# Other groups of the first weight loads, an order table solved anew, and two casts moved to GpSimd in an attention and MoE kernel

## The chip, the cores and the metric

The kernel runs on one core of one Trainium2 chip. The metric is the device time of one execution in microseconds (us). The time given for a kernel is the median of its runs. Before the change it was 302.77 us (three runs, 302.61 to 303.33). A difference below 2% (6 us) counts as "same".

## The reference, cut to what matters

```python
# q, k, v: 8 batches x 8 heads x 576 tokens x 64
q_s = softmax(q, axis=-1)              # over the 64 features
k_s = softmax(k, axis=2)               # over the 576 tokens
kv  = einsum('bhsd,bhse->bhde', k_s, v)
x   = einsum('bhsd,bhde->bhse', q_s, kv)      # then reordered to 4608 tokens x 512
h   = x @ w_in                         # 512 -> 2048   ("W1" in the kernel)
g   = where(h > 0, h, exp(min(h, 0)) - 1)
out = g @ w_out                        # 2048 -> 512   ("W2")
```

(The reference subtracts the maxima ahead of the exponentials; the kernel, with its small inputs, does not.)

## The kernel before: what the change and the argument touch

The attention is worked in 16 *units* (a batch, and half of its heads), the MoE in 9 *blocks* of 512 tokens. For a unit ScalarE takes the exponentials of q and k and casts v to bf16 (tile VB); VectorE sums and scales q (tile QS); q is transposed (tile qsT, by TensorE for the first units, by a DMA afterwards); TensorE makes kv (VB and k), VectorE normalizes it into MBLK, TensorE multiplies qsT with it, and the result is copied to XT, the input of the MoE. For a block TensorE multiplies XT with W1, ScalarE (ESB) and VectorE (ESB, GT) work out the ELU, TensorE multiplies GT with W2, and ScalarE or VectorE copies the result to an output buffer (OSB) from which it is stored.

All operations are created in program order and numbered. In what order an engine executes them is not decided when the program runs: it is a fixed table of those numbers, one row for each engine.

```python
BYDMA = 4
CASTS = 4
ORDER = {
    "pe":  ("30 28 32 45 43 47 50 68 54 67 70 71 69 72 82 86 93 103 115 128 90 129 ..."),
    "act": ("3 22 33 23 31 24 34 29 44 35 48 55 73 76 77 79 83 84 87 94 95 104 97 ..."),
    # ... rows for VectorE, GpSimd and the queue of SyncE ("sp")
}
```

A small model of the machine walks through the table. It decides one thing only: where TensorE is thought to idle after 9.4 us, and how many *warm-up* matmuls (128x128, on the identity, result unused) are put there.

```python
SPIN_FROM = 9400.0
def fill(self, seq):
    out, free, done = [], self.SPIN_FROM, False
    for o in seq:
        if o.eng == "pe" and not done:
            idle = o.start - free - 150
            count = int(idle / 80)
            if count > 1 and all(d.end < free for d in self.spare_after):
                # ... an op of `count` warm-up matmuls, which waits for the identity alone
            free = o.end
            done = o is self.spare_until
        out.append(o)
```

The loads of W1 (groups of 256 columns; the first groups cut into two halves of the contraction), the casts, and the output buffers:

```python
for g0, g1, half in ((0, 3, 0), (0, 3, 1), (3, 5, None), (5, 8, None)):
    self.load_w1(g0, g1, half, -30, [gate, self.ident] if half == 0 else ())

def first(n, what="qk"):                    # the first work of unit n
    def go():
        self.stage1(n, due(n), what=what, vconv="gp" if n < CASTS else "act")
        # ...

def widen(self, n, key):                    # qsT of unit n from its transposed bf16 form
    # ...
    if n < CASTS:   # on GpSimd
        # ...
    else:           # on ScalarE

def out_store(self, jb, ts, bk, key, eng="act"):
    if jb == 0:
        i, osb = f"x{ts}", self.OSB0[ts]    # block 0: four buffers of its own (OSBX)
    else:
        i = self.oslot % len(self.OSB)      # afterwards a ring of three (OSB)
        # ... copy the bank to the buffer, then two stores of 64 rows (128 KB) each
```

`widen` is only called for units from `BYDMA` = 4 on, so its GpSimd branch was never taken. The q, k and v loads of the later units and the stores are issued by one engine, SyncE, in the order of the table's row "sp".

The softmax here doesn't subtract the row's maximum and nothing guards it: scores larger than these inputs give would overflow.

## Time and profile before

| | before |
|---|---|
| median of 3 runs | 302.77 us |
| profiled run, span in the trace | 302.01 us, 300.2 us |
| first transpose on TensorE | 8.91 us |
| full clock rate, by the trace's clock record | 11.94 us |
| first W1 matmul | 15.42 us |
| last matmul starts | 296.27 us |

In the profile PE is TensorE, DVE VectorE, ACT ScalarE, POOL GpSimd, SPq the queue of DMAs that SyncE issues. "L545" is a line of the program. As the matmuls are issued by helper functions, it pays to learn five of them: L406 transposes, L458 kv, L489 attention output, L545 W1, L590 W2; L655 are the warm-ups. After the change the same lines are L403, L456, L487, L543, L588 and L653. A *hole* below is the time by which the starts of two neighbouring matmuls lie further apart than is usual for that shape (0.227 us for 128x512); it is about 0.16 us larger than the idle time that the profile reports, since the record of one such matmul lasts 0.39 us (those of before just ahead of 53 us), longer than the usual step to the next start.

Two lines of the page of the kernel before: the busy time of each engine, and the chain of waits that ended last.

```profile
PE 286.4 (95%) x1855; PEld 234.2 (78%) x1855; DVE 189.0 (63%) x244; ACT 182.7 (61%) x213; POOL 20.2 (7%) x31
...
PE 88%; ACT 6%; DMA 3%; DVE 2%; issue 0%; SPq 0%
```

TensorE is the bound: it is busy for 95% of the span, and 88% of the last chain is its own work. Then its waits between 15 and 280 us (who waits for whom: us in all, how often, longest).

```profile
PE PS L545 <- ACT OSBX L607: 0.6, 1, 0.6
PE PS L458 <- ACT XT L511: 0.4, 1, 0.4
```

After the start-up there is 0.6 us to be had, at one place. That place and the start-up in TensorE's timeline (start, duration, what; in brackets the idle time ahead of it and what ended it), first at 8 to 16 us:

```profile
8.91 1.14 PE L406 MATMUL PS<-ID,QS 128*128 128x128 f16 x9 [8.91 <-DVE QS L383]
9.84 2.13 PE L655 MATMUL PS<-ID 128*128 128x128 f16 x18
...
12.32 0.68 PE L406 MATMUL PS<-ID,QS 128*128 128x128 f16 x9
...
15.42 0.74 PE L545 MATMUL PS<-XT,W 128*128 128x512 f32 x2
```

Nine transposes took 1.14 us at 8.91 and 0.68 us at 12.32, their starts 107 and 56 ns apart: in between, at 11.94, the full rate of the clock record begins. And at 52 to 61 us:

```profile
52.28 1.07 PE L545 MATMUL PS<-XT,W 128*128 128x512 f32 x4
53.90 3.94 PE L545 MATMUL PS<-XT,W 128*128 128x512 f32 x16 [0.55 <-ACT OSBX L607]
...
59.13 0.78 PE L458 MATMUL PS<-VB,KR 64*64 64x65 bf16 x72
```

The 0.55 us wait for ScalarE's copy of block 0's output (a hole of 0.71 us) is the largest after the start-up. The kv product of units 4 and 5 follows at 59.13.

### The profile page before, as it was taken

To read this page: it belongs to the slowest core of one execution; us is meant where nothing else is said; L and a number is where in the kernel's file an instruction comes from. 1 tells how busy PE (TensorE), PEld (TensorE's weight loads), DVE (VectorE), ACT (ScalarE), POOL (GpSimd) and SP (SyncE) were. 2 spreads that over 40 slices of the span, in tenths; PEclk is the share of its full clock that TensorE was granted. 3 is DMA by queue.
4 is the path that set the end of the run, shared out by engine and by line. 5 is a ranking of instruction groups with operands and counts; after the bars stand their busy time and mean duration, and the time that the engine had idled before them with its cause. 6 is when DMAs were issued, how large, how long until landed. Compare 5 with 4: busy or idle time off the path is not lost.

```text
span 300.2 us, 4428 instructions
## 1 busy us (share of the span) xinstructions
PE 286.4 (95%) x1855; PEld 234.2 (78%) x1855; DVE 189.0 (63%) x244; ACT 182.7 (61%) x213; POOL 20.2 (7%) x31
## 2 busy tenths in 40 slices
PE   0799999999999999999999999999999999999995
PEld 0678887777888888888888878888888888888883
DVE  3858934987896596787687567675344546356500
ACT  5858759988976889668937664555441543233311
POOL 0950343000000000000000000000000000000000
PEclk9999999999999999999999999999999999999998
DMA  7999999795769697368477730324030032111133
GB/s 265 385 400 388 391 340 328 232 215 211 214 154 330 177 244 218 81 213 291 131 174 180 212 114 2 75 57 107 0 86 2 0 72 60 27 36 36 35 88 87
DMA packets 35283, 49.96 MB, mean 166 GB/s; under 512 B 16320, under 2 KB 16320, under 8 KB 35264
## 3 DMA queue, kind: packets, MB, share of 16 engines
q1 hardware_dynamic: 29680, 34.09, 41.1%
q0 software_dynamic: 5504, 15.47, 15.9%
q8 instruction: 14, 0.23, 0.3%
q10 hardware_dynamic: 80, 0.13, 0.1%
q14 instruction: 5, 0.04, 0.0%
HBM read 36.70 MB, written 9.44 MB: 154 GB/s over the span
## 4 chain that ended last, share of the span: by engine, by line
PE 88%; ACT 6%; DMA 3%; DVE 2%; issue 0%; SPq 0%
PE PS L590 41%; PE PS L545 41%; PE PS L489 3%; PE PS L458 2%; DMA out_dram<-OSB 2%; ACT QR L355 1%; DMA QR<-in_q_dram 1%; ACT ESB L561 1%; PE PS L406 1%; ACT VB L368 1%; ACT KR L359 1%; PE PS L655 1%; ACT OSB L607 1%; DVE QS L383 0%; DVE ZQ L375 0%; ACT XT L511 0%
## 5 line engine op out<-in xcount | busy, mean ns | idle before, releaser
L590 PE MATMUL PS<-W,GT 128*128 128x512 f32 x576 | 141.7, 392 | 0.0
L545 PE MATMUL PS<-XT,W 128*128 128x512 f32 x576 | 140.4, 392 | 0.7 <-ACT OSBX L607 0.6
L545 PEld LDWEIGHTS PS<-XT,W 128*128 128x128 f32 x576 | 106.8, 188 | 24.4 <-ACT OSBX L607 1.0
L590 PEld LDWEIGHTS PS<-W,GT 128*128 128x128 f32 x576 | 106.6, 188 | 22.2 <-ACT OSB L607 0.6
L561 ACT ACTIVATE ESB<-PS 128x1024 f32<-128x1024 f32 x72 | 73.6, 1027 | 64.5 <-PE PS L545 64.4
L578 DVE TENSOR_SCALAR ESB<-ESB 128x1024 f32<-128x1024 f32 x64 | 44.1, 690 | 70.6 <-ACT ESB L561 70.4
L580 DVE TENSOR_TENSOR GT<-ESB,PS 128x1024 fp32r<-128x1024 f32 x64 | 77.6, 1218 | 1.7
L607 ACT ACTIVATE OSB<-PS 128x512 f32<-128x512 f32 x32 | 18.8, 598 | 23.6 <-PE PS L590 19.0
L511 ACT ACTIVATE XT<-PS 128x512 fp32r<-128x512 f32 (+6 forms) x32 | 19.3, 607 | 15.3 <-PE PS L489 13.9
L375 DVE TENSOR_REDUCE ZQ<-QR 128x18 f32<-128x1152 f32 x16 | 21.5, 1346 | 6.0 <-ACT QR L355 6.0
L383 DVE TENSOR_TENSOR QS<-QR,RZQ 128x1152 f16<-128x1152 f32 x16 | 21.7, 1355 | 0.3
L355 ACT ACTIVATE QR<-QR 128x1152 f32<-128x1152 f32 x16 | 18.4, 1166 | 3.0 <-DMA QR<-in_q_dram 3.0
L359 ACT ACTIVATE KR<-KR 128x1152 bf16<-128x1152 f32 x16 | 18.6, 1163 | 1.2 <-DMA KR<-in_k_dram 1.2
L434 ACT ACTIVATE qsT<-QT 128x1152 fp32r<-128x1152 f16 x12 | 14.0, 1170 | 3.3 <-DMA QT<-QS 2.7
L368 ACT ACTIVATE VB<-VR 128x1152 bf16<-128x1152 f32 (+1 forms) x14 | 15.9, 1132 | 0.0
L489 PE MATMUL PS<-qsT,MBLK 128*128 128x320 f32 (+5 forms) x64 | 14.0, 305 | 0.3 <-DVE MBLK L471 0.2
L489 PEld LDWEIGHTS PS<-qsT,MBLK 128*128 128x128 f32 x64 | 11.6, 189 | 3.4 <-DVE MBLK L471 0.6
L574 DVE SCALAR_TENSOR_TENSOR GT<-PS,ESB 128x1024 fp32r<-128x1024 f32 x8 | 9.8, 1222 | 3.0 <-ACT ESB L572 2.9
L406 PE MATMUL PS<-ID,QS 128*128 128x128 f16 x36 | 3.2, 243 | 8.9 <-DVE QS L383 8.9
L471 DVE TENSOR_TENSOR MBLK<-PS,RZK 64x128 fp32r<-64x128 f32 x32 | 9.2, 287 | 0.9
L406 PEld LDWEIGHTS PS<-ID,QS 128*128 128x128 f16 x36 | 2.4, 109 | 9.3 <-DVE QS L383 8.9
L572 ACT ACTIVATE ESB<-ESB 128x1024 f32<-128x1024 f32 x8 | 8.5, 1060 | 0.2
(28 smaller groups left out, 57.9 us busy)
## 6 DMA issues: line engine op xcount, KB each, us to landing
out_dram<-OSB SPq DMA_DIRECT2D x63, 128.0 KB, 2.4
QR<-in_q_dram SPq DMA_DIRECT2D x12, 576.0 KB, 4.7
KR<-in_k_dram SPq DMA_DIRECT2D x12, 576.0 KB, 5.1
VR<-in_v_dram SPq DMA_DIRECT2D x12, 576.0 KB, 5.2
W<-in_moe_w_out_dram POOLq DMA_DIRECT2D x4, 1024.0 KB, 16.1
QR<-in_q_dram POOLq DMA_DIRECT2D x4, 576.0 KB, 11.2
VR<-in_v_dram POOLq DMA_DIRECT2D x4, 576.0 KB, 7.5
KR<-in_k_dram POOLq DMA_DIRECT2D x4, 576.0 KB, 13.1
```

Source lines behind the costliest of these rows:

```text
L355: S.add("act", t_act(1152, False), lambda e: e.activation(flat(q), flat(q), AF.Exp), key - 3, X=[f"qR{i}"], follow=self.table)
L359: S.add("act", t_act(1152, False), lambda e: e.activation(ek[:, :, :, :].rearrange("p h c d -> p (h c d)"), flat(k), AF.Exp), key - 2, X=[ ...
L375: S.add("dve", t_dve(1152), lambda e: e.tensor_reduce(self.ZQ[i][:, :, :].rearrange("p h c -> p (h c)"), q[:, :, :, :].rearrange("p h c d ...
L383: S.add("dve", t_dve(1152), lambda e: e.tensor_tensor(qso, q[:, :, :, :], rz, ALU.mult), key - 3, R=[f"qR{i}", f"RZQ{i}"], W=[f"QS{self.al ...
L489: last = e.matmul(P[:, y:y + n_], M[:, f, :], T[:, c0:c1, f * 64:f * 64 + 64], start=True, stop=True)
L511: S.add("act", t_act((h1 - h0) * n_, True), lambda e, dst=dst, src=src: e.activation(dst, src, AF.Copy), key, W=W, X=X)
L545: last = e.matmul(P[:, t * 512:(t + 1) * 512], self.W1[:, kc, tt * 128:(tt + 1) * 128], self.XT[:, kc, rc:rc + BLK], start=(kc == 0), stop ...
L561: S.add("act", t_act(1024, True), lambda e: e.activation(esb[:, :], P[:, :], AF.Exp), key, W=[f"E{i}"], X=banks)
L578: S.add("dve", t_dve(1024, 2), lambda e: e.tensor_scalar(esb[:, :], esb[:, :], 1.0, -1.0, ALU.min, ALU.add), key, X=[f"E{i}"])
L580: S.add("dve", t_dve(1024), lambda e: e.tensor_tensor(gt, esb[:, :], P[:, :], ALU.max), key, R=[f"E{i}"], W=gw, X=banks)
L590: last = e.matmul(dst, GT[:, jj, ts * 128:(ts + 1) * 128], self.W2[:, jj, :], start=(jj == 0), stop=(jj == 15))
L607: S.add("act", t_act(512, True), lambda e: e.activation(osb[:, :], src, AF.Copy), key, W=[f"O{i}0", f"O{i}1"], X=[f"b{bk}"])
```

## The change

It loads W1 in groups 0-1, 2-4, 5-7 in place of 0-2, 3-4, 5-7, so that the first, small pieces land earlier. It puts the v casts of units 4 and 5 on GpSimd, which was 93% idle, to free ScalarE around 50 us. And the order table was solved anew with a scheduling model whose delays were set more closely. One effect is not seen in the diff: in the new model the first warm-ups, 16 of them, come to stand ahead of the first transpose instead of behind it.

```diff
-CASTS = 4
+CASTS = 6
 ORDER = {
     "pe": (
-        "30 28 32 45 43 47 50 68 54 67 70 71 69 72 82 86 93 103 115 128 90 129 130 138 137 107 131 "
+        "30 32 28 45 43 47 50 68 54 67 70 69 77 81 85 92 114 102 89 127 128 136 135 129 130 106 138 "
     # ... all the other rows of the table are replaced too
-    LAT = {"pe": 200, "act": 138, "dve": 116, "gp": 155}
+    OVER = {"pe": 163, "act": 105, "dve": 82, "gp": 110}
     # ... the delays of the model
 def widen(self, n, key):
-        if n < CASTS:
+        if n < 4:
 # ...
-        for g0, g1, half in ((0, 3, 0), (0, 3, 1), (3, 5, None), (5, 8, None)):
+        for g0, g1, half in ((0, 2, 0), (0, 2, 1), (2, 5, None), (5, 8, None)):
 # ...
-            for g in range(3):
+            for g in range(2):
                 self.hg_mm(0, g, turns[g], key, half)
-                S.ops[-1].follow = kv1
         for g in range(8):
-            self.hg(0, g, turns[g], key, "da"[g % 2], g > 2)
+            self.hg(0, g, turns[g], key, "da"[g % 2], g > 1)
```

The `widen` line only keeps the widening of units 4 and 5 where it was, on ScalarE. (One operation fewer is created at the start, so the numbers of all later ones shift; the two tables cannot be compared number by number.)

## The prediction

> **What bounds the kernel.** TensorE. The page gives PE 286.4 of 300.2 us busy; in the chain of waits PE holds 88%, mostly rows of 128x512 matmuls starting 0.227 us apart: 1152 x 0.227 = 261 us, which the change does not touch. Outside that: 8.9 us before the first transpose, 6.5 us of start-up (8.9 to 15.42, first W1 matmul), 3.5 us after the last matmul. From 62 us on PE idles 0.4 us in 235 (table of stretches); the largest hole after start-up is 0.55 us at 53.3, where PE waits for ScalarE's last OSBX copy. So little can be won: 1 to 1.5 us, far below 2% (6 us).
>
> **What the change does.** PE's work and the bytes stay equal. It moves:
>
> 1. *Start-up order.* VectorE now does both q sums first, then both scalings, so QS0 is ready one sum and one reciprocal later (1.35 + 0.27 us): the first transpose moves from 8.91 to about 10.55. QS1 stays at 11.85. The 16 warm-up matmuls now stand ahead of the first transpose and wait only for the identity: I expect them at 1.5 to 3.3 us, useless, with 7 us of idle behind them. Before, 18 of them filled 9.84 to 11.77, spaced 107 ns; spacing fell to 56 ns after the clock changed at 11.94 (clock record). [...] After, the fast clock should come 1 to 3.5 us later, at 13 to 15.5. ScalarE must do both halves of qsT0 after the second k exponential (0.6 + 0.7 us), then half of v1 (0.68), qsT1 (0.70) and XT (0.59): from 12.4 this gives XT at 15.7 to 16.0, so the first W1 matmul starts at 15.7 to 16.05. Cost 0.3 to 0.65 us.
>
> 2. *W1 groups.* The first half lands earlier (14.52 before, about 13.9 after), but no PE wait ended with it. Groups 2-4 should land at 19.5 to 20.6 and are needed at about 20.2: 0 to 0.4 us of stall.
>
> 3. *Blocks 0/1.* Block 1 begins on banks that ScalarE freed earlier; the hole at 53.3 [...] should vanish: -0.6.
>
> 4. *v casts of units 4, 5 on GpSimd.* Takes 2 x 1.16 us off ScalarE, which is busy 13.25 of 13.40 us there, but bounds nothing except the hole. GpSimd took 1.92 and 1.15 us for such casts. The kv product of units 4 and 5 moves from 59.1 to about 57.5 us and needs unit 5's cast by then: 0 to 0.4 us of new wait. The widening stays on ScalarE, as it was in effect.
>
> 5. *After 62 us.* Same work, other interleaving: within 0.4 us.
>
> **Sum.** +0.45 (start-up) +0.1 (W1) -0.6 (hole) +0.1 (kv) -0.3 (later): about -0.25 us of 302.77. I predict 302.5 us, 8 in 10 between 301.3 and 303.7; faster by over 2%: 0.01, within 2%: 0.98, slower by over 2%: 0.01.
>
> **What would show it.** PE's timeline: warm-up matmuls at 1.5 to 3.3 us; first transpose near 10.55, spaced 107 ns; first W1 matmul 15.7 to 16.05; no OSBX release in PE's waits near 53; kv of units 4/5 before 58 us; same 3.5 us tail.
>
> **What would make it wrong.** The fast clock only after 17 us (each slow 128x512 matmul would cost about 0.2 us more, worked out as twice the spacing); groups 2-4 a microsecond late; the GpSimd cast slowed so that kv waits; or ScalarE starting XT sooner, making start-up a gain and the total 301.5.

The +0.45 of the start-up is added up from durations on ScalarE, and the -0.6 is the hole. The range for the fast clock, 13 to 15.5 us, is the author's estimate: before's trace has 3.03 us from the first transpose (8.91) to the full rate (11.94), which with a first transpose at 10.55 gives 13.6; no trace before the result showed how wide the range should be. The 0.2 us for a slow matmul is an estimate too, from the usual 0.227 us and the spacings of 107 and 56 ns; later two 128x512 matmuls took 1.20 us ahead of the full rate (e1, at 14.19) where two took 0.73 us after it (before, at 13.32). And that the 16 warm-ups would be useless was expected, not shown; e6 below leaves them out.

## The result, and the profile after

| | before | after |
|---|---|---|
| median of 6 runs | 302.83 us (301.89 to 303.33) | 303.49 us (302.67 to 304.45) |
| profiled run, span | 302.01 us, 300.2 us | 302.98 us, 301.2 us |
| first transpose | 8.91 us | 10.29 us |
| full clock rate | 11.94 us | 13.46 us |
| first W1 matmul | 15.42 us | 15.28 us |
| last matmul starts | 296.27 us | 297.22 us |

The ratio is 1.0023, with a 95% interval of 0.9999 to 1.0047. Ratios in this document are the mean time of one kernel's fast runs over that of the other's of the same rounds, so not quite the ratio of the medians quoted. The time lies inside the predicted range, but the sign is wrong: -0.25 us was forecast and the medians differ by +0.66.

The same two lines of the page of the changed kernel:

```profile
PE 287.5 (95%) x1854; PEld 234.9 (78%) x1854; DVE 188.8 (63%) x244; ACT 182.0 (60%) x211; POOL 21.8 (7%) x33
...
PE 78%; DMA 8%; DVE 7%; ACT 5%; issue 1%; SPq 1%
```

TensorE's share of the last chain fell from 88 to 78%, DMA and VectorE gained: new waits lead into TensorE. Its waits between 15 and 280 us:

```profile
PE PS L487 <- DVE MBLK L469: 0.6, 2, 0.4
PE PS L588 <- DVE GT L578: 0.4, 1, 0.4
PE PS L487 <- ACT XT L509: 0.4, 1, 0.4
PE PS L543 <- DVE RZK L465: 0.3, 1, 0.3
```

The OSBX wait is gone, as intended; four others stand in its place. The start-up in TensorE's timeline:

```profile
1.54 1.89 PE L653 MATMUL PS<-ID 128*128 128x128 f16 x16 [1.54 <-POOL ID L293]
...
10.29 0.61 PE L403 MATMUL PS<-ID,QS 128*128 128x128 f16 x4 [6.86 <-DVE QS L380]
...
15.28 0.93 PE L543 MATMUL PS<-XT,W 128*128 128x512 f32 x3 [0.29 <-DVE RZK L465]
```

The warm-ups are where they were expected, with 6.86 us of idle behind them, and the first transpose is 1.4 us later. At 52 to 61 us:

```profile
51.67 3.35 PE L543 MATMUL PS<-XT,W 128*128 128x512 f32 x14
55.40 1.21 PE L588 MATMUL PS<-W,GT 128*128 128x512 f32 x4 [0.38 <-DVE GT L578]
56.67 2.10 PE L543 MATMUL PS<-XT,W 128*128 128x512 f32 x8
58.71 0.78 PE L456 MATMUL PS<-VB,KR 64*64 64x65 bf16 x72
```

The hole of 0.71 us at 53 has turned into one of 0.54 at 54.63 (TensorE waits for GT, the ELU result) and one of 0.24 at 56.21: 0.78 together. TensorE was 0.99 us ahead of before at 54.4, and level with it at 57 to 61.

Lining the two traces up at equal matmul work done shows where time comes from (after minus before, in us):

| place (time in the changed kernel) | difference |
|---|---|
| first W1 matmuls to 50 us | -0.15 |
| 54.4 us | -0.99 |
| 57 to 61 us | 0 |
| 75 to 100 us | -0.2 |
| after a hole of 0.52 at 99.84 | +0.4 |
| after a hole of 0.37 at 107.14 | +0.97 |
| 140 to 166 us | +0.8 |
| after a hole of 0.53 at 173.60 | +1.66, then +1.1 where before has its own hole (0.26 at 177.24) |
| last matmul | +0.95 |

So in these two traces everything is lost at three holes after 62 us, where I had expected the same work "within 0.4 us" (the -0.3 in the sum stands there without a reason). The chain of waits of the changed kernel that leads into the first two (start, duration, what):

```profile
90.92 6.78 DMA VR<-in_v_dram
97.70 0.02 issue
97.72 1.17 ACT VB L365
98.89 1.05 ACT KR L356
99.94 0.59 ACT XT L509
...
105.91 1.25 DVE QS L380
...
107.39 0.31 DVE MBLK L469
...
107.74 0.56 PE PS L487 x2
```

ScalarE's row of the table puts the v cast of a unit, the k exponential and only then the XT copy. The v load, issued at 90.92, landed 6.78 us later; ScalarE stood idle for 0.67 us in front of the cast, and the XT copy, whose input from TensorE had been ready since about 96.6, came two operations later. To the hole at 107 the chain runs on through an ELU exponential behind that copy and then through VectorE, whose row puts the sum and the scaling of a q (ZQ, QS) ahead of the normalization into MBLK for which TensorE waits. In this trace, then, the ready copy waited some 3 us (96.6 to 99.85), in part behind a cast that was not ready. The chain into the third hole:

```profile
162.86 6.55 DMA out_dram<-OSB
...
169.43 0.60 ACT OSB L605
...
172.76 1.22 DVE GT L578
...
174.01 0.31 DVE MBLK L469
...
174.36 0.56 PE PS L487 x2
```

The output buffer ring of three is full: ScalarE's copy at 169.43 needs a buffer whose store was issued at 162.86 and landed 6.55 us later. SyncE's timeline at 156 to 172 us shows what stood ahead of it.

```profile
159.22 0.89 SPq L315 DMA_DIRECT2D KR<-in_k_dram  x2
160.15 0.47 SPq L315 DMA_DIRECT2D VR<-in_v_dram  x1
160.68 0.73 SPq L615 DMA_DIRECT2D out_dram<-OSB  x1
161.46 1.36 SPq L419 DMA_TRANSPOSE QT<-QS  x1
162.86 0.59 SPq L615 DMA_DIRECT2D out_dram<-OSB  x1
```

Three loads of 576 KB were issued ahead of a store of 128 KB, with another store and a DMA transpose in between. The median of all 63 stores is 2.4 us from issue to landing (the page's section of DMA issues, in both kernels); this one took 6.55. The loads seem to be enough for such a delay: the store at 160.68, which has the three loads but no transpose right ahead of it, took 7.34. The larger part, though, was lost before the issue. ScalarE had filled this buffer by 150.54, and the other half of it was issued at 150.57; but the row puts this half behind the loads, and SyncE stood 8.2 us (its waits at 148 to 172 us) until TensorE's kv product of 158.38 let the first of them go. In e4 below, where the same store is issued ahead of the loads, it leaves at 151.28 and has landed at 154.21, 15.2 us earlier. In this trace the store landed, at 169.41, behind the loads issued ahead of it, which landed at 163.05, 164.78 and 167.61.

### The profile page after: what moved, and what is told of

The parts are those of the page before. It is cut to its first block, busy times and chain, and to the rows that moved or that the text cites. A ratio compares the mean times of both kernels' runs of the same rounds, so it can differ in the third digit from the quotient of the medians.

```text
span 301.2 us, 4424 instructions
## 1 busy us (share of the span) xinstructions
PE 287.5 (95%) x1854; PEld 234.9 (78%) x1854; DVE 188.8 (63%) x244; ACT 182.0 (60%) x211; POOL 21.8 (7%) x33
## 4 chain that ended last, share of the span: by engine, by line
PE 78%; DMA 8%; DVE 7%; ACT 5%; issue 1%; SPq 1%
PE PS L588 36%; PE PS L543 36%; DMA QR<-in_q_dram 3%; PE PS L487 3%; DMA VR<-in_v_dram 2%; DMA out_dram<-OSB 2%; DVE ZQ L372 2%; ACT ESB L559 2%; DVE GT L578 2%; PE PS L456 1%; DVE QS L380 1%; PE PS L403 1%; DVE ESB L576 1%; ACT QR L352 1%; ACT VB L365 1%
## 5 line engine op out<-in xcount | busy, mean ns | idle before, releaser
L380 DVE TENSOR_TENSOR QS<-QR,RZQ 128x1152 f16<-128x1152 f32 x16 | 22.4, 1404 | 0.1
L365 ACT ACTIVATE VB<-VR 128x1152 bf16<-128x1152 f32 (+1 forms) x12 | 13.5, 1124 | 1.7 <-DMA VR<-in_v_dram 1.7
```

The lines of the kernel that those rows point to most:

```text
L380: S.add("dve", t_dve(1152), lambda e: e.tensor_tensor(qso, q[:, :, :, :], rz, ALU.mult), key - 3, R=[f"qR{i}", f"RZQ{i}"], W=[f"QS{self.al ...
```

## The experiments

Eleven kernels were run on two chips, each beside the kernel before, all with correct results. Those of one group ran on the same chip, in the same rounds, and share the runs of the kernel before. After the result I held this theory: the late order of the queues costs the time, and the start-up gives a small gain. The rivals: the two traces are two draws, and the start-up, whose fast clock comes later, is what costs; or neither, and it is noise.

### Group 1: is it the late order, or the start-up?

Kernel before in this group: median 302.66 us (302.35 to 303.94, 11 runs).

**e1_again**: the changed kernel, unedited.

> The changed kernel once more, nothing edited. Queue theory (the time is lost after 62 us, where ScalarE and the store queue wait in order behind late DMA): the same three PE holes show again, about 0.5 us near 99.8, 0.4 near 107.1, 0.5 near 173.6, and the first W1 matmul starts at 15.2 to 15.5, no later than before's 15.42; ratio to before 1.001 to 1.004. Rival, chance: the holes move or go, and the ratio is within 0.001 of 1. Rival, late clock: the start of the first W1 matmul lies behind before's by 0.3 us or more.

Measured: 303.65 us (303.50 to 304.25, 5 runs), ratio 1.0032 [1.0014, 1.0050]. So the kernel is slower, by about 1 us; that is not noise. But its trace is not the first one again. The fast clock came at 16.72 us instead of 13.46, the first W1 matmul at 16.22 instead of 15.28, W1's groups 2-4 landed at 21.04 instead of 19.60 (a hole of 0.28 at 20.58), and of the late holes there were 0.39 at 108.01 and 0.38 at 174.48, and none near 100. The rival is true as well: of the traces with this start-up, the first had shown the earliest.

**e2_late_old**: the changed kernel; from about 62 us on every engine follows the order of the kernel before.

```diff
 "act": first part as in the changed kernel
-   ... 342 365 296 295 291 346 299 360 351 391 377 362 395 404 ...
+   ... 342 346 291 296 292 391 295 351 299 395 365 375 400 360 ...   # the old order, renumbered
# the other rows likewise
```

> Changed kernel, but each engine's order after about 62 us is that of the kernel before; start-up, W1 groups, GpSimd casts and blocks 0 and 1 stay new. Queue theory: no PE hole over 0.15 us after 62 us except perhaps before's 0.26 near 177; last matmul about 1 us earlier than in the changed kernel; ratio to before 0.998 to 1.000. Rival (start-up clock or GpSimd casts cost): the loss stays, ratio 1.002 or more.

Measured: 303.47 us (302.41 to 303.73, 6 runs), ratio 1.0014 [0.9993, 1.0034]. The holes at 100, 107 and 173 are gone (0.19 at 75.6 and 0.26 at 178.7 are left). For those at 107 and 173, which after and e1 both have, this speaks for the late order as their maker; the one at 100 was missing in e1 already, without any edit. The median is only 0.18 us below that of e1 and misses the expected 0.998 to 1.000: the start-up was again slow (clock 14.85, first W1 matmul 16.05), and TensorE waited for W1, with a hole of 0.62 (its timeline at 19 to 22 us):

```profile
18.80 1.77 PE L545 MATMUL PS<-XT,W 128*128 128x512 f32 x7
21.03 1.19 PE L545 MATMUL PS<-XT,W 128*128 128x512 f32 x4 [0.46 <-DMA W<-in_moe_w_in_dram]
```

**e3_late_new**: the other way round, the kernel before with the changed order from about 62 us on.

```diff
 "act": first part as before
-   ... 343 347 292 297 293 392 296 352 300 396 366 376 401 ...
+   ... 343 366 297 296 292 347 300 361 352 392 378 363 396 ...   # the new order, renumbered
# the other rows likewise
```

> Kernel before, but each engine's order after about 62 us is that of the changed kernel; start-up, W1 groups of 3+2+3, ScalarE casts stay old. Queue theory: PE holes near 99.8, 107 and 173 come with the late order, together 1 to 1.4 us; ratio to before 1.002 to 1.004. Rival (start-up or casts): ratio within 0.001 of 1, no such holes.

Measured: ratio 1.0022 [0.9999, 1.0046], five runs of 302.49 to 304.26 us. The profiled run (438.3 us at a mean granted clock of 0.63) is left out; so no trace shows its holes. e2 (early part changed, +0.14%) and e3 (late part changed, +0.22%) add up to about e1 (both, +0.32%); each alone has 1 just inside its interval, so how the 1 us divides between the start-up and the late order is not settled by them.

**e4_queue_fix**: the changed kernel with the five operations moved that the chains above had named: one XT copy ahead of the v cast and the k exponential that kept it waiting, and four stores ahead of three loads.

```diff
 "act":
-   365 296 295 291 346        # 296 v cast, 295 k exponential, 291 XT copy
+   365 291 296 295 346
 "sp":
-   480 458 506 476 477 467 520 534 507 535 494 519 578      # 476 477 467 loads
+   480 458 506 507 494 520 519 476 477 467 534 535 578      # 507 494 520 519 stores
```

> Changed kernel with five places moved: on ScalarE one XT copy (the one that ran at 99.85) goes ahead of the v cast and the k exponential that stood before it; on the SP queue four 64-row output stores go ahead of the k and v loads issued at 159 to 160 us. Queue theory: the XT copy ends near 97.8, the holes near 99.8 and, as its consequence, near 107.1 go, and the hole near 173.6 goes; last matmul 1.0 to 1.4 us earlier than in the changed kernel, ratio to before 0.997 to 1.000. If the hole near 107 stays it has a cause of its own (VectorE's order); if the one near 173.6 stays the stores were not its cause.

Measured: 302.27 us (301.62 to 302.60, 6 runs), ratio 0.9983 [0.9966, 1.0000]; 1.4 us below e1 of the same rounds. The holes at 100 and 173 are gone, 0.17 of that at 107 is left. TensorE's timeline at 172 to 176 us, first of the changed kernel, then of e4:

```profile
172.02 1.97 PE L588 MATMUL PS<-W,GT 128*128 128x512 f32 x8
174.36 0.56 PE L487 MATMUL PS<-qsT,MBLK 128*128 128x320 f32 x2 [0.37 <-DVE MBLK L469]
```

```profile
172.18 1.98 PE L590 MATMUL PS<-W,GT 128*128 128x512 f32 x8
173.99 0.52 PE L489 MATMUL PS<-qsT,MBLK 128*128 128x320 f32 x2
```

No idle time is noted there in e4. This was in spite of a late clock (16.34) and a first W1 matmul at 16.12. Five moved places thus turn the changed kernel from the slower of the two to one that is level or a little faster. The cause of the hole at 173 is settled: it stands in every fast trace with the four stores behind the loads (six kernels) and in none of the four kernels with them moved (e4, e9, e10, e11). That of the hole at 107 is not: it comes back with 0.37 us in e9 and e11, which have the same moves, and in e9 its chain leads from the late v cast and the k exponential over an ELU exponential and VectorE's order (QS ahead of MBLK), without the XT copy; e4's expectation had named this case. Nor do the traces show all of the 1.4 us: e4's last matmul starts 1.14 us before e1's, and 0.57 of that is there at 99 us already, ahead of the holes, where only the scatter between executions is seen. The part of the start-up was open.

### Group 2: what do the parts of the start-up cost?

Another chip; kernel before 302.99 us (302.40 to 304.25, 11 runs). All four are edits of the changed kernel, whose late order they keep.

**e5_w1_old**: the old grouping of W1's loads.

```diff
-        for g0, g1, half in ((0, 2, 0), (0, 2, 1), (2, 5, None), (5, 8, None)):
+        for g0, g1, half in ((0, 3, 0), (0, 3, 1), (3, 5, None), (5, 8, None)):
```

> Changed kernel with the W1 loads again by groups 0-2, 3-4, 5-7; its order and everything else stay. In three of four traces with the new grouping PE stood 0.2 to 0.6 us at 20.2 to 20.6 us for groups 2-4, which landed at 20.7 to 21.0. Theory that the grouping costs: that wait is gone and the ratio to before is 0.0005 to 0.002 lower than the changed kernel's 1.0032, i.e. 1.001 to 1.003; the late clock stays (fast clock after 13 us in most traces). Rival, grouping is innocent: ratio unchanged, or a new wait for the larger first half before the first W1 matmul.

Measured: 303.33 us (302.56 to 303.81, 6 runs), ratio 1.0005 [0.9984, 1.0026]. There is no wait near 20 us, as expected, although the clock (15.51) and the first W1 matmul (16.05) came late; the ratio is a little below the expected 1.001 to 1.003. Holes of 0.35 at 107.2 and 0.62 at 173.65 remain. In this trace the start-up is late with the old grouping too, so the new one is not needed to make it late; what it adds is the wait near 20 us, up to 0.6 us so far.

**e6_no_early**: without the 16 warm-ups at 1.5 us.

```diff
-                if count > 1 and all(d.end < free for d in self.spare_after):
+                if count > 1 and free > self.SPIN_FROM and all(d.end < free for d in self.spare_after):
```

> Changed kernel without the 16 warm-up matmuls that ran at 1.5 to 3.4 us; the ten later ones stay. If those 16 do nothing, as predicted (7 us of idle behind them), the fast clock comes as late as before, 13 to 17 us, and the ratio to before stays at 1.002 to 1.004. If they do help, the fast clock comes later still and the ratio goes over 1.004.

Measured: 304.60 us (303.44 to 306.47, 6 runs), ratio 1.0056 [1.0023, 1.0090]. The trace has the clock at 13.71 and the first W1 matmul at 15.69, within the spread of the kernels that do have them; a hole of 0.35 at 19.82 for W1; and a hole of 1.33 at 173.25. Two of the six runs had a granted clock of 0.992 to 0.994 and took 306.2 and 306.5 us; what lowered it is open (one run each of e7 and e8 shows the same). Nor is it the clock alone: another run took 305.29 us at a granted clock of 1.000. The profiled run is the fastest of the six, so no trace shows the slow ones, and I do not read the ratio as the price of the warm-ups.

**e7_warm**: 40 warm-ups in place of the 16, held back until the first q exponential has ended.

```diff
+                early = free == self.SPIN_FROM
+                count = 40 if early else count
# ...
+                    if early:
+                        p.deps[self.ops[22]] = "raw"      # the first q exponential
```

> Changed kernel with 40 warm-up matmuls in place of those 16, and these wait for the first q exponential, so they run from 5.8 to at most 10.2 us, right up to the first transpose. Clock theory: fast clock at 8 to 11 us, transposes spaced 56 ns, first W1 matmul at 15.2 to 15.4 in every trace. But groups 2-4 of W1 still land at 20.6 to 21.0, so PE then waits for them 0.5 to 1 us at about 19.7 and only 0 to 0.4 us of the start-up loss comes back: ratio 1.002 to 1.003. Rival, clock alone: the whole start-up loss of about 1 us comes back, ratio 0.999 to 1.000.

Measured: 304.81 us (303.56 to 307.89, 6 runs), ratio 1.0067 [1.0029, 1.0106]. The mechanism worked: TensorE's timeline at 5 to 21 us.

```profile
5.99 4.26 PE L657 MATMUL PS<-ID 128*128 128x128 f16 x40 [5.99 <-ACT QR L356]
10.40 0.40 PE L407 MATMUL PS<-ID,QS 128*128 128x128 f16 x4
...
15.09 1.19 PE L547 MATMUL PS<-XT,W 128*128 128x512 f32 x4 [0.45 <-ACT XT L513]
...
20.45 0.73 PE L547 MATMUL PS<-XT,W 128*128 128x512 f32 x2 [0.82 <-DMA W<-in_moe_w_in_dram]
```

The clock was full at 9.92, the first W1 matmul came at 15.09, and then the gain ran into W1's groups 2-4, which landed at 20.41: a hole of 0.98 at 19.25. In this trace the gain is lost in that hole and in one of 1.39 at 173.30. That does not explain the ratio, which is worse than that of e1: the profiled run is again the fastest of six (303.56), and no trace shows the slower ones.

**e8_warm_w1**: both, the held-back warm-ups and the old grouping.

```diff
+                count = 40 if early else count            # and the wait, as in e7_warm
-        for g0, g1, half in ((0, 2, 0), (0, 2, 1), (2, 5, None), (5, 8, None)):
+        for g0, g1, half in ((0, 3, 0), (0, 3, 1), (3, 5, None), (5, 8, None)):
```

> Both: the 40 gated warm-up matmuls and the old W1 grouping, else the changed kernel. If clock and grouping hide behind each other, only this one gets the start-up back: first W1 matmul at 15.2 to 15.4, no wait near 20 us, 16 W1 tiles done about 1.2 us earlier than in the repeat of the changed kernel; ratio to before 0.998 to 1.000 (the late holes remain). Rival: no better than the better of the two alone.

Measured: 303.58 us (302.94 to 305.03, 6 runs), ratio 1.0021 [0.9998, 1.0044]. Clock 10.14, first W1 matmul 14.75; but with three groups in each half the second half landed at 17.81, too late for so early a start: a hole of 0.88 at 16.95. And the third late hole grew to 1.85 us. Its chain:

```profile
161.90 7.92 DMA out_dram<-OSB
...
170.34 1.16 ACT qsT L435
...
174.77 0.57 PE PS L491 x2
```

This is what the group taught that I had not looked for. The store that frees the output buffer lands at nearly the same date in all of them. In the traces of all six kernels with the changed late order (after, e1, e5, e6, e7, e8) it landed at 169.41, 170.14, 169.56, 169.85, 169.96 and 169.82, and TensorE went on between 174.36 and 175.09, whatever it had gained before: the hole was 0.38 to 1.85 us wide. A start-up gain is swallowed there. The loads ahead of the store were issued over a wider range than that, 158.31 (e8) to 160.10 (e1), as they follow a kv product of TensorE; why the landing varied by 0.7 us only is open. The swallowing explains why e7 and e8 were no faster than the changed kernel, and it says that a gain can hardly be seen in a kernel with that hole. It does not explain why e6 and e7 came out slower than they should have been without any gain (1.0056 and 1.0067, where 1.002 to 1.004, if the 16 warm-ups do nothing, and 1.002 to 1.003 were expected); that stays open.

### Group 3: start-up and casts on top of the mended order

Same chip; kernel before 302.95 us (302.36 to 303.70, 11 runs).

**e9_fix_w1**: e4 with W1 in groups 0-1, 2, 3-4, 5-7, so that group 2 does not wait for 3 and 4.

```diff
-        for g0, g1, half in ((0, 2, 0), (0, 2, 1), (2, 5, None), (5, 8, None)):
+        for g0, g1, half in ((0, 2, 0), (0, 2, 1), (2, 3, None), (3, 5, None), (5, 8, None)):
# and the tables renumbered, as two loads are added
```

> The kernel with the five moved places (ratio 0.9983), and W1 loaded by groups 0-1, 2, 3-4, 5-7, so that group 2 has loads of its own. The clock is left late. Theory that group 2's wait costs and is no longer swallowed near 173 us: group 2 lands before 18 us, no wait near 20 us, the 0.2 to 0.4 us come back, ratio to before 0.997 to 0.998. Rival: the late clock alone sets the start-up, ratio stays at 0.998 or more.

Measured: 302.44 us (301.54 to 303.10, 6 runs), ratio 0.9983 [0.9966, 1.0001], that of e4. No wait near 20 us, clock at 16.62, first W1 matmul at 16.09; but the hole at 107 is there again (0.37 at 107.82). No gain of the grouping alone is shown while the clock is late.

**e10_fix_w1_warm**: e9 with 38 held-back warm-ups.

```diff
+                count = 38 if early else count            # and the wait, as in e7_warm (operation 24 here)
```

> As the one before, and 38 warm-up matmuls that wait for the first q exponential in place of the 16 early ones. Theory (clock and W1 both hold the start-up, and the store queue near 173 us swallowed the gain in the kernels where it was not mended): fast clock near 10 us, first W1 matmul at 14.7 to 15.2, no wait near 20 us, no hole over 0.3 us near 173, last matmul 0.8 to 1.3 us earlier than in the kernel with the five moved places (296.8), ratio to before 0.993 to 0.996. Rival (nothing is gained by an early clock, since another fixed date comes later): ratio as of the kernel without these warm-ups, 0.997 or more.

Measured: 301.77 us (301.09 to 303.46, 7 runs), ratio 0.9957 [0.9944, 0.9971]. This beats both kernels, by 0.4% over before. The clock was full at 8.85, the first W1 matmul came at 15.13, and neither a wait near 20 nor the hole at 173 is there; TensorE's timeline at 170 to 178 us:

```profile
171.53 1.99 PE L595 MATMUL PS<-W,GT 128*128 128x512 f32 x8
173.35 0.51 PE L494 MATMUL PS<-qsT,MBLK 128*128 128x320 f32 x2
```

Its last matmul starts at 296.16, 0.64 us before that of e4 (296.80) where 0.8 to 1.3 was expected, and 1.14 us before that of e9. Of this 1.14 about 0.5 us is the start-up's (it is there at 62 us) and 0.44 arises between 101 and 108 us, where e9 has its hole at 107.82 and e10 has none; why it has none is not shown. The profiled run is its slowest of seven: its span of 300.2 us equals that of before's lucky trace, so the gain rests on the other six (spans 299.3 to 300.0) against the runs of before in the same rounds, not on the comparison of two traces. A small hole for W2 (0.24 at 32.92) and those at 55 and 57 (0.55 and 0.24) are left.

**e11_fix_casts**: e4 with the v casts of units 4 and 5 back on ScalarE, placed by hand in its row.

```diff
-CASTS = 6
+CASTS = 4
 "act":
-   146 153 204 175 229 230 187 233 179
+   146 153 180 204 175 229 230 187 233 188 179      # 180, 188: the casts
 "gp":
-   144 180 185 188
+   144 185
```

> The kernel with the five moved places, and the v casts of units 4 and 5 back on ScalarE, put where ScalarE is about when their data land (after the two XT copies of block 1, and ahead of the k exponential of unit 4). If the GpSimd casts are worth nothing: the kv product of units 4 and 5 runs at 58.5 to 59.5 us as before and the ratio stays at 0.998. If they are worth something: ScalarE stands waiting for v, kv slips to 60 us or later, a PE hole of 0.3 to 1 us shows at 55 to 60 us, ratio 0.999 to 1.002.

Measured: 304.36 us (303.62 to 305.39, 6 runs), ratio 1.0054 [1.0035, 1.0072]. So it was slower than the 0.999 to 1.002 that were expected even if the casts mattered. The kv product of units 4 and 5 slipped to 60.91; of TensorE's waits between 15 and 280 us the two largest are these:

```profile
PE PS L458 <- ACT KR L358: 0.8, 1, 0.8
PE PS L545 <- DMA W<-in_moe_w_in_dram: 0.8, 1, 0.8
```

The first is the cost of the casts: the k exponential of unit 5 came behind its cast and ended too late (hole 0.99 at 59.69). The second is the lateness of W1 again (hole 0.95 at 19.70), some 30 us ahead of these casts. So in this order, and with this one placing by hand, the casts on ScalarE cost about a microsecond; other placings were not tried. It does not follow that the move is a gain by itself: before, with its own order and the casts on ScalarE, had the same kv product at 59.13 without a hole.

## Why the prediction was right or wrong, point by point

**Bound and size: right.** TensorE's matmuls bound both kernels; all differences are under 0.7%.

**Step 1, start-up, +0.45: right in mechanism, about right in size; one trace alone would have misled.** First transpose 10.29 (10.55 forecast), warm-ups at 1.54 with idle behind them, the later clock. The seven traces with this start-up (after, e1, e2, e4, e5, e9, e11) have the first W1 matmul at 15.28 to 16.22, median 16.05, at the upper end of the forecast 15.7 to 16.05, and the full clock at 13.46 to 16.72 where 13 to 15.5 was forecast. The trace taken right after the change is the earliest in both. There ScalarE's five copies and casts ran from 12.22 to 15.08, 2.86 us, where I had added up durations of 3.27: it starts the next operation about 0.1 us before the recorded end of the one before.

| kernel | full clock | first W1 matmul | W1 groups 2-4 landed |
|---|---|---|---|
| before | 11.94 | 15.42 | (other groups) |
| after | 13.46 | 15.28 | 19.60 |
| e1_again | 16.72 | 16.22 | 21.04 |
| e2_late_old | 14.85 | 16.05 | 20.98 |
| e4_queue_fix | 16.34 | 16.12 | 20.69 |
| e5_w1_old | 15.51 | 16.05 | (old groups) |
| e9_fix_w1 | 16.62 | 16.09 | (own groups) |
| e11_fix_casts | 13.91 | 15.54 | 20.83 |
| e7_warm | 9.92 | 15.09 | 20.41 |
| e10_fix_w1_warm | 8.85 | 15.13 | (own groups) |

Of before's start-up there is a single fast trace, that of a quick run (302.01 us, where its median is 302.83), so how much of the 0.66 us is the start-up's is not settled to a tenth.

**Step 2, W1 groups, +0.1: mis-sized.** Groups 2-4 were forecast to land between 19.5 and 20.6; they landed between 19.60 and 21.04, and the hole was 0 (after), 0.28 (e1), 0.62 (e2), 0.17 (e4), 0.35 (e6) and 0.95 us (e11), where 0 to 0.4 was forecast. In the first trace they were needed at 19.65 and had just landed, at 19.60; a start-up as late as e1's hides part of a late landing. The gain that was to pay for it, the earlier first half, met no wait of TensorE, as forecast.

**Step 3, the hole at 53, -0.6: failed.** "[T]he hole at 53.3 [...] should vanish." The OSBX wait did vanish; but two holes of 0.54 and 0.24 us stand at 54.63 and 56.21, where TensorE is ahead and waits for the ELU of block 1 on VectorE. Net +0.07 instead of -0.6; the two stand in the ten traces after, e1, e2 and e4 to e10 alike (0.54 to 0.55 and 0.23 to 0.26). I had priced the wait that was removed and not asked which wait came next behind it.

**Step 4, casts on GpSimd, +0.1: right that they bound nothing, right on the wait, wrong on the date.** They took 1.15 us each, and the kv product had no wait; but it came at 58.71, not before 58, as the holes of step 3 pushed it back. e11 suggests that the place of the kv product in the new order hangs on them.

**Step 5, after 62 us, -0.3: failed.** "Same work, other interleaving: within 0.4 us." The same work in another order cost TensorE three holes, 1.42 us together in the first trace, 0.77 in e1. e2 removes them all, e4 those at 100 and 173; e4, with five moved operations, is 1.4 us faster than e1, of which its trace shows some 0.6 at the late holes. What the table had done: put a v cast that depends on a DMA in front of a ready copy, and three big loads, for which SyncE had to wait, in front of a store that frees an output buffer. Step 3 and step 5 each missed by enough to turn the sign alone.

In the sum +0.45 +0.1 -0.6 +0.1 -0.3 = -0.25, the terms -0.6 and -0.3 came out at about +0.07 and between +0.5 (e1's two late holes, 0.77, less before's own of 0.26) and +1.15 (the lag in the first trace, from -0.2 ahead of the first late hole to +0.95 at the end), so the kernel was a little slower where a little faster was said. That the start-up cost nothing (-0.15) in the first trace was, by the later ones, the luck of that execution. The range held since the effects are small, not since all steps were right.

**What stays open.** How before's start-up scatters, and with it how the loss divides between the start-up and the late order; what makes the hole at 107 come and go; what slowed several runs of e6, e7 and e8, and lowered the granted clock in some of them; why the landing of W1 varies by 1.4 us between traces.

## What to carry to other kernels

When an order is solved anew, look in the new order for operations that wait for a DMA and stand ahead of ready work on the same engine, and for small transfers that free a buffer and stand in the queue behind large ones, above all behind ones that themselves have to wait: here such a store was issued 12 us after its data were ready. Moving five such places made the kernel 1.4 us faster, by the medians, than the unedited repeat. A gain ahead of a wait whose end does not move with it (here a store that landed at 169.4 to 170.1 us in six kernels) cannot be seen in the total, so mend the last such wait first and measure the earlier changes on top of it. And take the start-up from several traces: the full clock rate came anywhere between 13.46 and 16.72 us with the same start-up order.

## What else the traces showed

- From the start of TensorE's work to the full clock rate it took 3.0 us in before (transposes from 8.91, full rate from 11.94). With the changed start-up order, active from 10.3 us on but for short waits, it took 3.2 us (after, 10.29 to 13.46) to 6.3 us (e1, 10.44 to 16.72), and from the first held-back warm-up 3.9 us in e7 (5.99 to 9.92) and 2.9 us in e10 (5.92 to 8.85). What sets it is not shown.
- Transposes ran faster after the full rate had begun: nine took 1.14 us before it and 0.68 us after it (before, at 8.91 and 12.32), and four took 0.61 us before it (after, at 10.29) and 0.40 us after it (e7, at 10.40).
- 128 KB stores behind three 576 KB loads took 7.34 and 6.55 us (the second with a DMA transpose ahead of it as well) instead of the median of 2.4 (after).
- A cast on GpSimd took 1.92 us (before, at 34.54) when a VectorE multiply (QS from QR and RZQ) had begun first, at 34.10, and 1.15 us at 44.28, where VectorE was idle. Such a multiply took 2.26 us (after, at 34.24) when a cast had begun first, at 34.15, and 1.36 us at 40.54 without a cast.
- One execution on one core, at a mean granted clock of 0.63, took 438.3 us instead of 303 (e3, one run of six).
